# Attention on 64-row halves: another queue for the query blocks, other constants for the side work, other orders of passes and adds

## The chip, the core and the metric

The kernel runs on one core of a Trainium2 chip. A core has TensorE for matrix products (PE in the profile, its weight loads PEld), VectorE (DVE), ScalarE (ACT), GpSimd (POOL) and SyncE (SP), each with an instruction queue of its own that is worked off in order. The metric is the device time of one launch in microseconds (us). The kernel before took 2493.73 us, the median of three runs (2489.62 to 2493.9).

## The reference

Three stages in a row, on u and v of shape 4 x 3072 x 256 and z of shape 4 x 3072 x 64:

```
attn = maximum((1/3072) * z @ z.T, 0) ** 2        # per batch, 3072 x 3072, symmetric
x    = u * (attn @ v)
x    = (h - tanh(h)) @ w_out,  h = x @ w_in       # w_in 256 x 2048
k    = maximum(xk @ w_k, 0) ** 2                  # xk, xr mix x with its row before
out  = sigmoid(xr @ w_r) * (k @ w_v)              # w_k 256 x 1024
```

All weights come as 64-bit floats. Products have single precision: each operand is split into a high part (rounded to TensorE's float format) and a low part (the rest), and every product is three passes, high x high, high x low, low x high.

## The kernel before

The diff touches only the attention stage. It works through 24 tiles t of 512 queries: batch b = t // 6, block g = t % 6. A tile has 12 units p = 0 to 11 (counted through, n = 12 t + p, 288 in all), each for two blocks of 128 keys.

A **fresh** unit computes its scores (`score`, 6 matmuls of 64 rows: two row halves of the array, which run side by side), then `square` on ScalarE (relu, square), a high copy h_A (ScalarE, line 89) and a low part l_A = a - h_A (VectorE, line 92). As the attention matrix is symmetric, a fresh unit whose key block lies beyond the query block is also kept: VectorE transposes it (k, line 660) and SP stores it (at). A **repeated** unit has no scores: `again_load` (line 689, four DMAs on SP) brings a stored block b back, `again_high` (line 700) makes the high part h_t on ScalarE, `produce` the low part l_t on VectorE. Block g has 2 g repeated units; their places stand in a table (`rrfrrrrrfrrr` for g = 5, r repeated, f fresh).

`consume` then adds attn @ v into four accumulators in PSUM: 24 matmuls a unit, two for each (j, c, n), with j one of two key blocks, c one of two column halves, n the pass. The pass n = 1 reads the low part of the unit; passes 0 and 2 its high part. A unit is consumed two units after its scores (LAG = 2, line 56). At the end of a tile the four accumulators have to be emptied before the next tile may write them: `x1_add` (line 1223) copies one half on ScalarE and adds the other on VectorE (both write xs), once for each c; it is handed to `produce` of the next tile's unit p = 1.

The order on every queue is that of the program text, unit by unit: `begin(n)` issues the loads registered for slot n, then scores of unit n, consume of unit n - 2, produce of unit n, the high part of unit n + 1 if it is repeated, and side work. Loads on SP: u of a tile (`u_load`, 8 DMAs, transposing, slot 12 t + 1, or 12 t - 7 where g = 5), the tile's queries q (`ask`, line 148, 8 DMAs of 64 KB each, slot 12 t - 5; only the scores read them), the stored blocks b (five units ahead of their first use), v, z, and the 64-bit weights c.

Side work is spread by a planner, `run_steps` (line 1405), which runs once a unit: in a fresh unit on VectorE between the square and the low part, in a repeated one after the low part. Each task has a first unit, a last unit and steps with costs in us: the conversion of each piece of a 64-bit weight (25 pieces in turn, 4 steps of 1.7, 1.7, 1.2 and 1.5, its load three units before its first unit), transposes of u (1.1), products with u (1.3), splits of v (a ScalarE copy and 1.3) and of z (1.0). A unit has a credit of 2.0, less 1.4 at p = 1 and less 1.0 in a repeated or 1.1 in a kept unit. Steps run while the credit is above zero, and regardless of it when a task has reached its last unit; what is overdrawn is carried on to the next unit.

After the attention, two feed-forward stages run on full 128-row matmuls; GpSimd issues transfers with addition for them.

Of the kernel before, what the change touches and what calls it, by code (L numbers as in the profile page):

```python
# [19 lines left out]
def relu2_attention__tanh_ffn__channel_mix_kernel(  # L20
# [23 lines left out]
    nc = tc.nc  # L44
# [4 lines left out]
    DC = D // P  # L49
    NG = S // TB  # L50
    NT = B * NG
    NP = S // (2 * P)
# [3 lines left out]
    LAG = 2  # L56
# [15 lines left out]
    def p2(name, dt=F32, n=512):  # L72
        return sb.tile([P, n], dt, tag="p2", name=name, bufs=NG + 7)
# [17 lines left out]
    def sub_lo(o, i, hi):  # L91
        nc.vector.tensor_tensor(out=o, in0=i, in1=hi.bitcast(F32), op=ALU.subtract)  # L92
# [55 lines left out]
    def ask(t):  # L148

        b, g = divmod(t, NG)  # L150
        w = asks[t] = [p2(f"q{t}_{l}", F32R) for l in range(2)]
        for l in range(2):
            for d in range(2):
                for h in range(2):
                    nc.sync.dma_start(
                        out=w[l][d * DQ : (d + 1) * DQ, h * 256 : (h + 1) * 256].bitcast(F32),
                        in_=keys[b, g][l][h * DQ : (h + 1) * DQ].bitcast(F32),
                    )
# [475 lines left out]
    def square_split(name, w, sc, high, beside, a, adds):  # L634
        a = a or scratch(f"a_{name}")
        h, l = parts(name)
        square(a, w, sc, adds)
        beside(a)
        high(h, a)
        sub_lo(l, a, h)  # L640
        return h, l
# [3 lines left out]
    for g, order in enumerate(  # L645
        ("ffffffffffff", "ffffrfrfffff", "fffrfrffrffr", "frfrfrfrfrfr", "rrfrfrrfrrfr", "rrfrrrrrfrrr")
    ):
        left = {"r": list(range(2 * g)), "f": list(range(2 * g, NP))}
# [5 lines left out]
    def keep(n, b, g, kp, a):  # L654


        def turn():
            st["t"] = t = p4(f"k{b}_{g}_{kp}", shape=(P, 4, 4, 2, 32))
            for c in range(2):
                nc.vector.transpose(  # L660
                    out=t[:, :, :, c].rearrange("p b a j -> p a b j"),
                    in_=a[:, c].rearrange("p (a b i) -> p a b i", a=4, b=4),
                )

        def store():
            t = st["t"]
            rows = kept[b, g, kp // 2][kp % 2 * P : (kp % 2 + 1) * P, :]
            nc.sync.dma_start(out=rows, in_=t.rearrange("p b a c j -> p (b a c j)"))
            stored.add((b, g, kp))

        st = {}
        if later(n):
            task(n + 3, n + (7 if n < 4 else 9), lambda: [(1.3, turn), (0.0, store)])
        else:
            turn()
            stores[n + 1] = store
# [3 lines left out]
    def wide(n):  # L680
        if n // 2 not in wides:
            wides[n // 2] = sb.tile([P, 2, 2, 512], F32, tag="big", name=f"a_A0_{n}", bufs=12)
        return wides[n // 2][:, n % 2]

    def later(n):

        return 2 <= n < NP
# [128 lines left out]
    def produce(unit, w, adds):  # L816
        kind, t, p = unit
        name = f"{kind}{t}_{p}"
        n = at[unit]
        if n in turned:  # L820
            views, split[unit] = turned.pop(n)
            for hj, lj, xj in views:
                sub_lo(lj, xj, hj)
            for f in adds:
                f()
            return
        b, g = divmod(t, NG)
        kp = pairs[g][p]
        kept_on = (b, g, kp // 2) in kept

        def beside(a):
            run_steps(n)
            if kept_on and not later(n):
                keep(n, b, g, kp, a)

        a = wide(n) if later(n) and kept_on else None
        split[unit] = square_split(
            name, w, scale,
            nc.vector.tensor_copy if not n // NP and n % 2 else copy_hi, beside, a, adds,
        )  # L840
        if kept_on and later(n):
            keep(n, b, g, kp, a)

    def get_acc(kind, t):
        if (kind, t) not in acc:
            acc[kind, t] = [
                ps.tile([P, 512], F32, tag="acc", name=f"acc_{kind}{t}_{c}", bufs=2 * DC)
                for c in range(2 * DC if kind == "A" else DC)
            ]
        return acc[kind, t]  # L850

    def consume(unit):
        for f in pieces_of(unit):
            f()

    def pieces_of(unit):
        kind, t, p = unit
        s = split.pop(unit)
        o = get_acc(kind, t)
        last = NP - 1  # L860
        w = []
        for j in range(2):
            f = 2 * p + j
            kp = pairs[t % NG][p]
            f = kp // 2 * 4 + kp % 2 + 2 * j
            w.append([vs[t // NG, f // 4][:, l, f % 4] for l in range(2)])
        order = [(j, c, n) for j in range(2) for c in range(DC) for n in range(3)]
        if unit == units[0]:
            order = [(j, c, n) for j, n in ((0, 0), (0, 2), (0, 1), (1, 0), (1, 2), (1, 1)) for c in range(DC)]
        elif unit in units[1 : NP - 1]:  # L870
            q = (0, 1, 2) if unit == units[2] else (0, 2, 1)
            order = [(j, c, n) for n in q for j in range(2) for c in range(DC)]
        elif p in (0, last):
            order = [(j, c, n) for c in range(DC) for n in range(3) for j in range(2)]
        whole = at[unit] >= NA - LAG

        def one(j, c, n):

            a, m = PASSES[n]
            for r in (slice(0, P),) if whole else (slice(0, DQ), slice(DQ, P)):  # L880
                nc.tensor.matmul(  # L881
                    o[c if r.start else DC + c],
                    w[j][a][r, c * P : (c + 1) * P],
                    s[m][r, j],
                    start=p == 0 and j == 0 and n == 0,
                    stop=p == last and j == 1 and n == 2
                    or bool(r.start) and at[unit] == NA - LAG - 1 and j == 1 and n == 2,
                )

        return [lambda x=x: one(*x) for x in order]  # L890
# [370 lines left out]
    def load(n, f, *args):  # L1261
        loads.setdefault(max(n, 0), []).append(lambda: f(*args))
# [6 lines left out]
    def task(first, last, steps, *args):  # L1269
        tasks.append([last, first, len(tasks), steps, args])  # L1270
# [3 lines left out]
            load(2 * g - 5, z_load, 0, g)  # L1274
        load(2 * g - 4, v_load, 0, g)
    for t in range(NT):
        n = t * NP + (-7 if t % NG == NG - 1 else 1 if t else 5)
        load(n, u_load, t)
        task(n + 5 if t else NP - 1, t * NP + NP, u_steps, t)
        if t:  # L1280
            load(t * NP - 5, ask, t)
        if t < NT - 1:
            task(t * NP + NP + LAG, t * NP + NP + LAG + 3, x1_steps, t)
    for b in range(1, B):
        prev = (b - 1) * NG * NP
        last = prev + (NG - 1) * NP
        for g in range(NG):
            n = last + LAG + (-18, -6, 3, 6, 9, 11)[g]
            load(n, v_load, b, g)
            task(n + 3, min(n + 12, b * NG * NP + 2 * g + LAG - 2), v_steps, b, g)  # L1290
        for g in range(NG):
            n = prev + 2 * NP + 7 * g
# [6 lines left out]
    order = [(k, g) for g in range(F1 // 512) for k in ("in", "out")]  # L1299
# [4 lines left out]
    for n, x in enumerate(halves):  # L1304
        k = c0 + n * (c1 - c0) // len(halves)
# [13 lines left out]
    for s in range(2):  # L1319
        n = last - 42 + 6 * s  # L1320
# [11 lines left out]
    n = NA + 3 * NHF + 2  # L1332
    load(n, lambda: half_load("ks", *[wd["k", g][:, h] for g in range(2) for h in range(2)]))
    task(n + 1, n + 5, ksum_steps)
    n = NB
# [22 lines left out]
    for i in range(NT // 2):  # L1358
        n = NA + NHF * i
        load(n - 7 if i else n - 18, x_load, i)  # L1360
        task(n - 6 if i else n - 14, n - 1 if i else n - 5, x_steps, i)
    for i in range(NT // 2):
        n = NB + (NK + 1) * i
# [31 lines left out]
    for k in range(8):  # L1395
        t, c, n = NT - 1 - k // 4, k // 2 % 2, NB + (NK + 1) * (k + 1)
# [6 lines left out]
    ready, spare, now = [], [0.0], [0]  # L1403

    def run_steps(n):
        now[0] = n
        for x in [x for x in tasks if x[1] <= n]:
            tasks.remove(x)
            ready.append((x[0], list(x[3](*x[4]))))
        ready.sort(key=lambda x: x[0])  # L1410
        kind = units[min(n, len(units) - 1)][0]
        left = {"A": 2.0, "S": 1.7, "K": 0.0}[kind] + spare[0]
        if kind == "A":
            t, q = divmod(n, NP)
            j = pairs[t % NG][q] // 2 - t % NG
            left -= 1.4 if q == LAG - 1 else 0.0
            left -= 0.3 if later(n) else 1.0 if j < 0 else 1.1 if j > 0 else 0.0
        while ready and (left > 0 or ready[0][0] <= n):
            for x in list(ready):
                if left > 0 or x[0] <= n:  # L1420
                    cost, f = x[1].pop(0)
                    f()
                    left -= cost
                    if not x[1]:
                        ready.remove(x)
        spare[0] = min(left, 0.0) if kind == "A" else max(min(left, 0.0), -0.8)

    with tc.manual_schedule():
        z_load(0, 0)
# [48 lines left out]

        rooms("ps_h")
        q = [f for u in units[NA - LAG : NA] for f in pieces_of(u)]  # L1480
        rest = q[-6:] + [f for cost, f in x1_steps(NT - 1)]
        q = q[:-6]
        for n, (L, i, j) in enumerate(seq):
            begin(slot(n))
            h_unit(n, q)
            q = rest + h_queue(n)
            rest = []
            if L == "K" and j == NK - 1:
# [6 lines left out]
                q = h_piece(n, 0, 0) + q[6:]  # L1495
        n = len(seq) - 1
        c11, c12, c22, c21 = q[:6], q[6:12], q[12:], h_piece(n, 1, 0)
        c21[-1] = with_out(c21[-1], n, 0)
        q = c12[:3] + c22[:3] + c12[3:] + c22[3:] + c11[:3] + c21[:3] + c11[3:] + c21[3:]
# [34 lines left out]
```

## Time and profile before

| | |
|---|---|
| median of 3 runs | 2493.73 us (2489.62 to 2493.9) |
| profiled execution | 2496.21 us, span 2494.3 us, granted clock 0.993 |
| PE, DVE, ACT, POOL busy | 98%, 79%, 76%, 10% of the span |

The profile is of one execution. "Busy" is the union of an engine's instructions; L12 is line 12 of the kernel; out<-in names the tiles written and read; the engine or DMA after "<-" in a wait is what ended it. PEclk is the granted share of TensorE's clock.

### The profile page before, as it was taken

What the parts mean: (1) busy time and instruction counts of PE and PEld (TensorE: products, weight loads), DVE (VectorE), ACT (ScalarE), POOL (GpSimd) and SP (SyncE); (2) the same over time, 40 slices, a digit from 0 to 9 for tenths busy, and PEclk for the clock granted to TensorE, in tenths of its full rate; (3) what the DMA queues carried; (4) which work ended last, traced back from release to release, by engine and by line L of the source; (5) the groups of instructions that cost most, each with busy time, mean ns of one, the idle gap of its engine ahead of it and who ended that gap; (6) DMA issues with size and microseconds to landing.
All of it is one profiled execution on the core that took longest, in us unless ns stands there. A gap on an engine that the chain in (4) does not pass through costs nothing.

```text
span 2494.3 us, 38956 instructions
## 1 busy us (share of the span) xinstructions
PE 2455.3 (98%) x14648; PEld 2026.6 (81%) x14648; DVE 1968.1 (79%) x2746; ACT 1906.8 (76%) x2562; POOL 242.4 (10%) x314
## 2 busy tenths in 40 slices
PE   9999999999989999999999999999999999999998
PEld 7788788778778887888888888888888888888887
DVE  8887888688778877777777777777778778878877
ACT  8765886588568767778777877777777888888886
POOL 0000000000000000022222212221222000000100
PEclk9999999999999999999999999999999999999999
DMA  6888588868877993155665556555667454445733
GB/s 184 245 225 215 185 223 211 215 191 230 206 208 245 258 243 113 39 94 114 144 144 99 112 123 127 109 107 118 127 127 166 138 131 115 114 126 131 160 108 71
DMA packets 447757, 389.39 MB, mean 156 GB/s; under 512 B 261328, under 2 KB 359120, under 8 KB 447568
## 3 DMA queue, kind: packets, MB, share of 16 engines
q1 hardware_dynamic: 395856, 310.67, 44.0%
q0 software_dynamic: 45888, 75.51, 18.9%
q8 instruction: 115, 1.88, 0.3%
q10 hardware_dynamic: 5824, 0.72, 0.2%
q14 instruction: 74, 0.61, 0.1%
HBM read 225.58 MB, written 199.48 MB: 170 GB/s over the span
## 4 chain that ended last, share of the span: by engine, by line
PE 87%; DVE 4%; DMA 3%; ACT 2%; SPq 1%; issue 1%; DVEq 0%; ACTq 0%
PE acc_A L881 23%; PE acc_H L938 21%; PE wa L901 16%; PE we L901 12%; PE acc_K L938 10%; PE w_A L724 3%; DMA b<-at 2%; PE wa_r L901 1%; DVE l_A L92 1%; DVE l_t L92 1%; PE we_q L901 1%; SPq L207 1%; ACT a_A L630 1%; DVE k L660 1%; ACT a_A L627 0%
## 5 line engine op out<-in xcount | busy, mean ns | idle before, releaser
L881 PE MATMUL acc_A<-h_A,v 64*128 64x512 f32 x2688 | 466.6, 390 | 2.4 <-DVE xs L1231 1.4
L881 PE MATMUL acc_A<-h_t,v 64*128 64x512 f32 (+1 forms) x1904 | 352.7, 393 | 16.6 <-ACT xs L1229 8.4
L881 PEld LDWEIGHTS acc_A<-h_A,v 64*128 64x128 f32 x2688 | 312.5, 186 | 54.8 <-DVE xs L1231 4.6
L881 PE MATMUL acc_A<-l_A,v 64*128 64x512 f32 x1344 | 307.1, 392 | 11.2 <-DVE l_A L92 11.1
L881 PEld LDWEIGHTS acc_A<-h_t,v 64*128 64x128 f32 (+1 forms) x1904 | 256.1, 188 | 56.6 <-DVE xs L1231 10.9
L627 ACT ACTIVATE a_A<-w_A 128x1024 f32<-128x1024 f32 (+1 forms) x169 | 171.9, 1017 | 124.6 <-PE w_A L724 123.8
L938 PE MATMUL acc_H<-h_Hy,w_out 128*128 128x512 f32 x768 | 263.9, 389 | 0.0
L881 PE MATMUL acc_A<-l_t,v 64*128 64x512 f32 (+1 forms) x952 | 255.1, 393 | 0.5 <-DVE l_t L92 0.5
L938 PE MATMUL acc_H<-h_Hx,w_out 128*128 128x512 f32 x768 | 252.2, 389 | 0.0
L901 PE MATMUL wa<-xo_T,w_in 128*128 128x512 f32 x864 | 242.8, 389 | 0.4 <-DVE rc L1038 0.4
L92 DVE TENSOR_TENSOR l_A<-a_A,h_A 128x1024 fp32r<-128x1024 f32 (+1 forms) x169 | 201.5, 1192 | 28.6 <-ACT h_A L89 27.9
L89 ACT ACTIVATE h_t<-b 128x512 fp32r<-128x512 f32 x240 | 136.7, 619 | 102.5 <-PE acc_A L881 60.0
L881 PEld LDWEIGHTS acc_A<-l_A,v 64*128 64x128 f32 x1344 | 172.0, 186 | 42.0 <-DVE l_A L92 17.6
L660 DVE STREAM_TRANSPOSE k<-a_A 128x512 f32<-128x512 f32 x240 | 155.6, 688 | 59.2 <-ACT a_A L630 59.0
L1004 DVE TENSOR_TENSOR r<-we,r 128x512 f32<-128x512 f32 x144 | 99.5, 691 | 125.9 <-PE we L901 84.6
L1164 POOL DMA_DIRECT2D mixd<-far x48 | 48.6, 1012 | 1519.3 <-ACT far L1161 1519.3
L1038 DVE TENSOR_TENSOR rc<-we,rc 128x512 f32<-128x512 f32 x144 | 99.3, 689 | 119.1 <-PE we L901 83.3
L901 PEld LDWEIGHTS wa<-xo_T,w_in 128*128 128x128 f32 x864 | 162.0, 188 | 34.8 <-DVE rc L1038 1.3
L630 ACT ACTIVATE a_A<-a_A 128x1024 f32<-128x1024 f32 (+1 forms) x169 | 178.5, 1056 | 5.0
L92 DVE TENSOR_TENSOR l_Hy<-g_H,h_Hy 128x1024 fp32r<-128x1024 f32 x144 | 175.5, 1218 | 7.1 <-ACT h_Hy L89 5.2
L92 DVE TENSOR_TENSOR l_Hx<-g_H,h_Hx 128x1024 fp32r<-128x1024 f32 (+1 forms) x145 | 175.5, 1210 | 3.6 <-ACT h_Hx L89 2.4
L911 ACT ACTIVATE g_H<-rc 128x1024 f32<-128x1024 f32 x96 | 101.8, 1061 | 96.9 <-DVE rc L1038 95.9
(256 smaller groups left out, 5823.7 us busy)
## 6 DMA issues: line engine op xcount, KB each, us to landing
at<-k SPq DMA_DIRECT2D x120, 512.0 KB, 4.5
b<-at SPq DMA_DIRECT2D x240, 256.0 KB, 6.3
timed<-mixd POOLq DMA_DIRECT2D x144, 256.0 KB, 5.4
mixd<-own SPq DMA_DIRECT2D x96, 256.0 KB, 2.0
mx_T<-timed SPq DMA_DIRECT2D x96, 256.0 KB, 4.6
mx_B<-mixd SPq DMA_DIRECT2D x72, 256.0 KB, 4.9
uin<-in_u_dram SPq DMA_DIRECT2D x192, 64.0 KB, 3.2
x1d<-uT SPq DMA_DIRECT2D x24, 512.0 KB, 3.9
```

What stands on the lines that cost most here:

```text
L89: nc.scalar.activation(out=o, in_=i, func=ACTF.Copy)
L92: nc.vector.tensor_tensor(out=o, in0=i, in1=hi.bitcast(F32), op=ALU.subtract)
L627: nc.scalar.activation(out=a, in_=w, func=ACTF.Relu, scale=sc)
L630: nc.scalar.activation(out=a, in_=a, func=ACTF.Square)
L660: nc.vector.transpose(out=t[:, :, :, c].rearrange("p b a j -> p a b j"), in_=a[:, c].rearrange("p (a b i) -> p a b i", a=4, b=4),)
L724: nc.tensor.matmul(o[j], lhsT, asks[t][PASSES[k][1]][r], start=k == 0, stop=k == 2)
L881: nc.tensor.matmul(o[c if r.start else DC + c], w[j][a][r, c * P : (c + 1) * P], s[m][r, j], start=p == 0 and j == 0 and n == 0, stop=p == ...
L901: nc.tensor.matmul(o, w[l], x[m], start=first and k == 0, stop=last and k == 2, skip_group_check=True,)
L911: nc.scalar.activation(out=g, in_=h, func=ACTF.Tanh)
L938: nc.tensor.matmul(o[c], w[a][:, f % 4, c * P : (c + 1) * P], hp[n, half, t][m], start=bool(first and k == 0), stop=bool(last and k == 2),)
L1004: nc.vector.tensor_tensor(out=r1, in0=e, in1=r1, op=ALU.add)
L1038: nc.vector.tensor_tensor(out=rc[:, k], in0=x, in1=rc[:, k], op=ALU.add)
```

## The change

The eight DMAs of `ask` go from SP's queue to GpSimd's. In `produce`, a repeated unit that carries the tile-end adds issues add, low part, add, low part, in place of low part, low part, add, add. In `pieces_of`, units p = 1 to 10 (from tile 1 on) run all high x high products of the unit first, then those with its low part, then those with the low part of v; before, the three passes of one (j, c) followed each other. The load of u for the last block of a batch moves from slot 12 t - 7 to 12 t - 9, and its transpose's first unit with it. In the planner the deduction at p = 1 falls from 1.4 to 1.0, that of a repeated unit from 1.0 to 0.75, and in the attention at most 2.0 of debt is carried on.

```diff
@@ ask @@
-                    nc.sync.dma_start(
+                    nc.gpsimd.dma_start(
                         out=w[l][d * DQ : (d + 1) * DQ, h * 256 : (h + 1) * 256].bitcast(F32),
                         in_=keys[b, g][l][h * DQ : (h + 1) * DQ].bitcast(F32),
                     )
@@ produce @@
             views, split[unit] = turned.pop(n)
-            for hj, lj, xj in views:
+            for k, (hj, lj, xj) in enumerate(views):
+                for f in adds[k : k + 1]:
+                    f()
                 sub_lo(lj, xj, hj)
-            for f in adds:
-                f()
             return
@@ pieces_of @@
-        order = [(j, c, n) for j in range(2) for c in range(DC) for n in range(3)]
+        order = [(j, c, n) for n in range(3) for j in range(2) for c in range(DC)]
@@ loads and tasks @@
-        n = t * NP + (-7 if t % NG == NG - 1 else 1 if t else 5)
+        n = t * NP + (-9 if t % NG == NG - 1 else 1 if t else 5)
         load(n, u_load, t)
         task(n + 5 if t else NP - 1, t * NP + NP, u_steps, t)
@@ run_steps @@
-            left -= 1.4 if q == LAG - 1 else 0.0
-            left -= 0.3 if later(n) else 1.0 if j < 0 else 1.1 if j > 0 else 0.0
+            left -= 1.0 if q == LAG - 1 else 0.0
+            left -= 0.3 if later(n) else 0.75 if j < 0 else 1.1 if j > 0 else 0.0
@@ run_steps, at its end @@
-        spare[0] = min(left, 0.0) if kind == "A" else max(min(left, 0.0), -0.8)
+        spare[0] = max(min(left, 0.0), -2.0) if kind == "A" else max(min(left, 0.0), -0.8)
```

## Rows read from the trace of the kernel before

**Rows 1.** The page: span, and its part 1 (busy us, share, instructions).
```profile
span 2494.3 us, 38956 instructions
...
PE 2455.3 (98%) x14648; PEld 2026.6 (81%) x14648; DVE 1968.1 (79%) x2746; ACT 1906.8 (76%) x2562; POOL 242.4 (10%) x314
```
**Rows 2.** Chain of waits in order of time: start, us, engine, tile, line, instructions.
```profile
54.48 5.44 PE acc_A L881 x48
```
**Rows 3.** Windows: stretch, length, busy us and instructions by engine, clock, DMA share, GB/s.
```profile
10.00:951.00 941.00, 911.02 (x7826) 752.91 (x7826) 770.68 (x1115) 693.15 (x816) 0.00 (x0) 0.98 0.81 220
...
195.00:225.00 30.00, 27.00 (x222) 23.26 (x220) 21.11 (x35) 13.96 (x21) 0.00 (x0) 0.94 1.01 255
435.00:465.00 30.00, 24.40 (x170) 18.13 (x168) 16.48 (x29) 10.28 (x18) 0.00 (x0) 0.83 1.04 247
680.00:710.00 30.00, 22.36 (x174) 17.65 (x172) 17.69 (x29) 12.10 (x20) 0.00 (x0) 0.83 1.02 243
...
93.00:108.00 15.00, 12.93 (x101) 10.32 (x99) 11.91 (x18) 7.89 (x10) 0.00 (x0) 0.89 0.79 187
291.00:306.00 15.00, 12.71 (x98) 10.75 (x97) 12.21 (x18) 9.30 (x12) 0.00 (x0) 0.89 0.31 123
534.00:549.00 15.00, 12.69 (x100) 10.24 (x98) 12.20 (x18) 9.29 (x12) 0.00 (x0) 0.89 0.31 123
...
130.00:140.00 10.00, 8.61 (x75) 6.83 (x73) 7.90 (x11) 5.69 (x8) 0.00 (x0) 1.00 0.72 146
```
**Rows 4.** Waits of PE, 10 to 951 us: releaser, total us, times, longest.
```profile
PE acc_A L881 <- DVE l_A L92: 11.1, 9, 2.3
PE acc_A L881 <- DVE xs L1231: 9.6, 5, 4.5
```
**Rows 5.** Timeline of SP's queue, tiles 10 and 16: start, us to issue all.
```profile
416.36 3.33 SPq L694 DMA_DIRECT2D b<-at  x4
419.73 10.07 SPq L207 DMA_DIRECT2D uin<-in_u_dram  x8
...
430.38 4.95 SPq L155 DMA_DIRECT2D q<-z  x8
435.43 2.04 SPq L694 DMA_DIRECT2D b<-at  x4
...
655.87 0.46 SPq L232 DMA_DIRECT2D c_k<-in_moe_w_k_dram  x1
```
**Rows 6.** Timeline of ACT, tiles 10, 11 and 16; in brackets its idle time.
```profile
427.91 1.15 ACT L89 ACTIVATE h_t<-b 128x512 fp32r<-128x512 f32 x2 [1.19 <-PE acc_A L881]
428.97 1.05 ACT L89 ACTIVATE v<-vr 128x1024 fp32r<-128x1024 f32 x1
...
433.46 1.06 ACT L89 ACTIVATE h_A<-a_A 128x1024 fp32r<-128x1024 f32 x1
...
444.15 2.19 ACT L89 ACTIVATE h_t<-b 128x512 fp32r<-128x512 f32 x4 [8.59 <-DMA b<-at]
...
656.21 1.06 ACT L630 ACTIVATE a_A<-a_A 128x1024 f32<-128x1024 f32 x1
```
**Rows 7.** Timeline of PE: a fresh unit's start in tile 10; tile 16's fifth unit.
```profile
436.33 0.61 PE L881 MATMUL acc_A<-h_A,v 64*128 64x512 f32 x2
...
661.08 0.61 PE L881 MATMUL acc_A<-l_A,v 64*128 64x512 f32 x2
```
**Rows 8.** Timeline of DVE in tile 7: first of seven conversion instructions; l_A.
```profile
290.18 0.42 DVE L267 TENSOR_SCALAR c_in<-cw_in 128x512 int32<-128x512 int32 x1
...
295.44 1.18 DVE L92 TENSOR_TENSOR l_A<-a_A,h_A 128x1024 fp32r<-128x1024 f32 x1
```
**Rows 9.** Line 1164 on POOL: duration in ns, min/median/max; its landing.
```profile
L1164 POOL DMA_DIRECT2D mixd<-far x48: 858/870/2071, 1052.7 to 2306.3; - x48
...
DMA to landing us min/median/max: 3.9/4.2/7.4
```
**Rows 10.** DMA issues: KB each, median us to landing.
```profile
c_k<-in_moe_w_k_dram SPq DMA_DIRECT2D x4, 512.0 KB, 6.7
```

## The prediction

> **What bounds the kernel now.** I read the page's busy shares first: PE is busy 98% of the span, so only time in which PE waits or runs slowly can be won [rows 1]. A busy PE says little of its pace, so next comes the chain of waits, for the pace: 48 matmuls of the weighted sum in 5.44 us, 0.1133 us each when nothing is late [rows 2]. A repeated unit (24 matmuls) thus costs 2.72 us, a fresh one (30) 3.40. Then the windows, because they count matmuls: the length less 0.1133 us per matmul, plus 0.35 for the three that both edges count, is lost time. The attention stretch, 941 us with 7826 matmuls, lost 54.7 us [rows 3]. The diff touches nothing of the later stages, so this is all there is to win.
>
> Where it lies: the three windows around the starts of tiles 5, 11 and 17 (the last query block of a batch) lost 5.2, 11.1 and 10.6, together 26.9 [rows 3]. Three 15 us windows in tiles 2, 7 and 13 lost 3.9, 4.2 and 4.0, together 12.1; the window at tile 3's start 1.85 [rows 3]. The waits name the releasers: xs (the copies and adds that free the accumulators) for the first kind, l_A (the low part of a fresh unit) for the second, 11.1 us in nine waits, the longest 2.3 [rows 4]. Three long ones make about 6.9 of that; the other six add 4.2. In these windows the granted clock is 0.83 to 0.94 where other stretches have 1.00: after each long wait PE runs a while at the lower of its two levels (1.2 GHz), so a wait of 2.3 costs about 4 [rows 3, 4]. The remaining 9.6 us is crumbs, which I leave alone.
>
> The xs waits begin on SP. Ahead of tile 11 the queue issues eight transfers of u (10.07 us), eight of q (4.95) and only then the stored block b (ends 437.47) [rows 5]. ACT, in order, sits 8.59 us on that b before it can reach the xs copies behind it [rows 6]. While the eight q issue, nothing else can be issued, so every load behind them is 5 us late.
>
> **The change part by part.**
>
> *q by GpSimd.* SP loses 4.95 us of issue per tile in front of the b loads [rows 5]. GpSimd, which has no work in the stretch (POOL x0) [rows 3], gets eight DMAs. The trace has no such load there, so I bound it by the DMAs that it issues later: median 0.87, longest 2.07 us, landing 4.2 us after issue [rows 9]. At the median, 8 x 0.87 + 4.2 = 11.2 us, under the shortest five units of notice, 5 x 2.72 = 13.6: cost nothing. At the longest 20.8 us: 7.2 late. I take the median, as most rows lie at it. Nothing else is queued on GpSimd; only the scores of the tile's first fresh unit wait for q.
>
> The row shows VectorE and these DMAs side by side without harm in the later stages [rows 9]. The Trainium skill (SBUF — State Buffer, section "SBUF: two separate sides") speaks against the move: while VectorE runs a copy or cast that takes the port pair that both share, GpSimd can't write its descriptors, and its advice is to issue from SP or ACT; it gives about 3.1 us for a DMA of 0.62 overlapped so. By that figure eight take 24.8 us, an estimate, and q comes some 15 us late; no run here shows it in the attention stretch.
>
> *u two units earlier before tiles 5, 11, 17, 23.* This moves 10 us of SP issue too. Today the order is b (416.36, for the tenth and twelfth unit of tile 10), then u (419.73) [rows 5]. In slot -9 u passes in front of that b: u from 416.36 to 426.4, b to 428.5, and 6.7 us from the last issue to landing, as for the b of 437.47 that ACT got at 444.15 [rows 5, 6]: 435.2. ACT now starts on it at 427.91, so ACT is 7.3 late; a v copy of 1.05 behind it moves to an earlier unit, 6.2 remain; the next fresh unit's high part, done at 434.52, is wanted at 436.33, a lead of 1.8 [rows 6, 7]. New PE wait: 4.4 us. The same order stands at tiles 4 and 16. Bounds: nothing (if SP gets ahead) to 13.2, three times this; I take 7, as at tile 16 it hides behind the wait two paragraphs on. In return b for tile 11 issues by 430.5 and lands at 437.2, while ACT, late itself, asks at about 440: the 8.59 us wait goes. So do those of tiles 5 and 17. Of the 26.9 I keep 1.0 for the accumulators' own hand-over: -25.9, +7.
>
> *Side work spread.* I followed the planner's rule (the list of steps, their costs and due units) through all units, with the old and the new constants. With the old ones it puts three conversion steps (1.7, 1.2, 1.5) due at once into the third unit of tiles 2, 7 and 13; the trace has them in tile 7 from 290.18 on, and l_A of that unit only at 295.44 [rows 8]. The new constants give 120 repeated units 0.25 more and 24 tile ends 0.4 more, some 40 units of cost, and forgive debt beyond 2.0; after tile 0 no unit then gets more than 2.7, and no fresh unit whose block is kept more than 1.7. Total VectorE work is unchanged. The l_A waits go but for 1.5: 16.3 (12.1 + 4.2) less 1.5 is -14.8.
>
> Earlier work needs its data earlier. A conversion's load has three units of notice. At tile 16 the list now puts a z step and the first step of a c conversion into the fifth unit (before: the eleventh). That c load leaves SP at 655.87, behind u, z and b, and lands 6.7 us on (the median for it), at 662.6 [rows 5, 10]. VectorE reaches the step after the square, at 657.3 [rows 6], waits, then needs 1.5 for the step and 1.2 for l_A: 665.3. PE, with high passes first, wants l_A four slots into the unit, at 661.08 [rows 7]. That is 4.2, about 6 with the slow clock behind it. Three more such loads (tiles 5, 11, 17) end on repeated units with more lead; 1 together. Bounds of all these: 0 to 9. I take +7.
>
> *High passes first.* The low part is wanted at the fifth slot of twelve instead of the second, 3 x 0.227 = 0.68 us later; the number of matmuls and weight loads is the same. Taken alone it is worth up to 0.68 in each of nine waits, 5 us; with the bursts gone it only covers what is left, and is in the 1.5 above. The other half of a repeated unit's high part is wanted 0.9 us earlier: nothing while ACT leads by over 1 us.
>
> *Adds interleaved.* In blocks 3 to 5 the first add passes one half-width subtract on VectorE, the second also: each up to 0.7 sooner. That and u's transpose no longer sharing a unit with two steps take most of tile 3's 1.85: -1.4. In the other order a subtract waits behind an add that waits for PE; the unit that needs it starts a whole unit later, so nothing.
>
> **Sum.** 25.9 + 14.8 + 1.4 = 42.1 gone; 7 + 7 = 14 new: 28.1 less. The profiled execution took 2496.21 us (span 2494.3), the median shown is 2493.73; from the median: 2465.
>
> **The rivals.**
> A. The new waits stay away (SP, rid of q, is far enough ahead that u passes without making b late, and c lands in time). For it: the share of the DMA engines is below 1 over the whole stretch, 0.81 [rows 3]. Against: the q of this tile stands behind its u, not ahead of it [rows 5]. 2493.7 - 42 = 2452.
> B. The DMA engines, not SP, set when b lands: their share is 1.01 to 1.04 in the windows of tiles 5, 11, 17 [rows 3]. Then only half of 25.9 comes: 2465 + 13 = 2478. Against: a 5 us hole while q issues.
> C. Bursts move rather than go, since VectorE is 82% busy in the stretch (770.68 of 941) [rows 3]: the 14.8 shrinks to a couple: 2478.
> D, the other side: q late. It decides from 1.18 us per GpSimd DMA, (13.6 - 4.2) / 8. At the longest row, 2.07 us, q is 7.2 late in the 15 tiles whose first unit is fresh: 108 us, 2493.7 + 108 - 28 = 2574; 1.6 us each would still give 51 and end at about 2517. For it: new load on GpSimd beside a busier VectorE. Against: the median 0.87. By the figure that the Trainium skill gives (SBUF — State Buffer, above) it would end past 2574; no row here bears that out.
>
> **How the numbers follow.** Forecast 0.52, A 0.20, B 0.13, C 0.07, D 0.08. About 0.2% (5 us) is what a measurement of this kernel tells from no change. Forecast, A, B and C end below 2489 but for 0.05 in their tails, where more new waits come than I count: faster 0.87, same 0.05, slower 0.08. The range goes from A less some crumbs, 2447, to B with both new terms at their upper bounds, 2485.
>
> **What would show it.** Right: no q on SP and eight DMAs of about 0.9 us per tile on POOL; the windows at tiles 5, 11, 17 near 265 matmuls in 30 us (30 / 0.1133) with clock 1.00; no l_A wait of 2 us in tiles 2, 7, 13; a new ACT wait on b late in tiles 4 and 10, and a VectorE wait on c in tile 16. Wrong: w_A matmuls that wait for q at tile starts (D); xs waits at tile 11 of over 4 us (B); l_A waits elsewhere summing to 10 (C).

## The result, and the profile after

The changed kernel took 2460.89 us (median of 4, 2458.88 to 2462.69) against 2493.26 for the one before on the same chip (median of 4, 2489.62 to 2493.9): ratio 0.9873, 95% interval 0.9856 to 0.989, 32.4 us less. The forecast was 28 less. The profiled executions stand at 2496.21 before and 2462.35 after, 33.9 less, and it is these two that the rows compare.

First the page's span and its part 1, then the windows (columns as in [rows 3]), which answer to [rows 1] and [rows 3]:

```profile
span 2460.6 us, 39117 instructions
PE 2440.0 (99%) x14648; PEld 2037.7 (83%) x14648; DVE 1966.2 (80%) x2746; ACT 1908.6 (78%) x2562; POOL 338.1 (14%) x498
```
```profile
10.00:920.00 910.00, 898.70 (x7851) 765.48 (x7852) 770.55 (x1117) 697.40 (x820) 94.34 (x184) 0.99 0.83 228
...
190.00:220.00 30.00, 30.00 (x268) 24.77 (x266) 26.30 (x42) 18.75 (x27) 7.71 (x16) 1.00 1.10 280
415.00:445.00 30.00, 26.49 (x214) 21.26 (x212) 20.82 (x33) 17.21 (x25) 5.54 (x11) 0.98 1.10 273
660.00:690.00 30.00, 29.82 (x261) 24.34 (x259) 22.67 (x37) 18.95 (x28) 6.14 (x13) 1.00 1.07 277
628.00:658.00 30.00, 24.31 (x196) 20.27 (x194) 19.41 (x32) 14.34 (x19) 5.72 (x12) 0.89 0.94 226
...
93.00:108.00 15.00, 15.00 (x135) 14.20 (x133) 14.86 (x23) 11.69 (x14) 0.00 (x0) 1.00 0.76 226
290.00:305.00 15.00, 15.00 (x136) 12.40 (x134) 12.87 (x17) 12.34 (x13) 0.00 (x0) 1.00 0.59 187
528.00:543.00 15.00, 15.00 (x136) 13.26 (x134) 13.99 (x21) 13.84 (x14) 0.00 (x0) 1.00 0.94 270
...
126.00:136.00 10.00, 10.00 (x91) 10.00 (x89) 9.12 (x15) 7.26 (x10) 0.00 (x0) 1.00 0.93 195
```

Read as before, the attention stretch lost 910 - 7851 x 0.1133 + 0.35 = 20.8 us, where it had lost 54.7 [rows 3]: 33.8 less, the whole gain. The windows around the starts of tiles 5, 11 and 17 (second to fourth line) lost 0, 6.1 and 0.8 where they had lost 5.2, 11.1 and 10.6; the three in tiles 2, 7 and 13 and the one at tile 3's start lost nothing. Most of what is left lies in two places: 6.1 in the window of tile 11, and 30 - 196 x 0.1133 + 0.35 = 8.1 in a new one, 628 to 658, in tile 16, where the kernel before lost nothing. There the granted clock is 0.89; around the long waits before it was 0.83 to 0.94 [rows 3].

The waits of PE in this stretch (as in [rows 4]), the waits of VectorE on transfers, and four rows of VectorE's timeline name them:

```profile
PE acc_A L881 <- DVE l_A L92: 7.0, 4, 5.7
PE acc_A L881 <- DVE l_t L92: 2.4, 1, 2.4
PE acc_A L881 <- DVE xs L1231: 1.7, 4, 0.7
```
```profile
DVE cw_out L253 <- DMA c_out<-in_moe_w_out_dram: 10.2, 3, 5.8
DVE cw_k L253 <- DMA c_k<-in_moe_w_k_dram: 9.0, 2, 7.6
DVE zt L127 <- DMA zin<-in_z_dram: 2.4, 2, 2.0
```
```profile
403.93 0.43 DVE L253 TENSOR_SCALAR cw_out<-c_out 128x512 int32<-128x512 int32 x1 [2.81 <-DMA c_out<-in_moe_w_out_dram]
...
440.73 0.43 DVE L253 TENSOR_SCALAR cw_out<-c_out 128x512 int32<-128x512 int32 x1 [5.81 <-DMA c_out<-in_moe_w_out_dram]
...
637.74 0.43 DVE L253 TENSOR_SCALAR cw_k<-c_k 128x512 int32<-128x512 int32 x1 [7.63 <-DMA c_k<-in_moe_w_k_dram]
639.15 1.22 DVE L92 TENSOR_TENSOR l_A<-a_A,h_A 128x1024 fp32r<-128x1024 f32 x1
```

[Rows 4] show half of the waits on xs in the kernel before, those for VectorE (9.6); the copies on ScalarE held PE as well:

```profile
PE acc_A L881 <- ACT xs L1229: 8.4, 3, 4.0
```

Together the waits on xs fell from 18.0 to 1.7. In their place stand VectorE's waits on c: the conversion step now comes before the data. In tile 16 the low part l_A of that unit stands right behind the step, and PE waits 5.7 us for it. The one wait on l_t, 2.4 us, is tile 11's.

SP's queue and ScalarE in tile 10 (columns as in [rows 5] and [rows 6]):

```profile
397.57 10.05 SPq L207 DMA_DIRECT2D uin<-in_u_dram  x8
407.73 3.92 SPq L694 DMA_DIRECT2D b<-at  x8
...
413.07 3.89 SPq L108 DMA_DIRECT2D zin<-in_z_dram  x4
...
429.72 0.40 SPq L238 DMA_DIRECT2D c_out<-in_moe_w_out_dram  x1
...
629.15 0.45 SPq L232 DMA_DIRECT2D c_k<-in_moe_w_k_dram  x1
```
```profile
415.54 1.15 ACT L89 ACTIVATE h_t<-b 128x512 fp32r<-128x512 f32 x2 [6.99 <-DMA b<-at]
418.73 1.06 ACT L89 ACTIVATE h_A<-a_A 128x1024 fp32r<-128x1024 f32 x1
...
419.70 2.17 ACT L89 ACTIVATE h_t<-b 128x512 fp32r<-128x512 f32 x4
```

No q stands between u and b any more, and u passes in front of b, as the edit says. ScalarE's 8.59 us wait ahead of tile 11 [rows 6] is gone (the h_t at 419.70 starts without one), and a new one of 6.99 stands in tile 10, on the b that u passed.

### The profile page after: what moved, and what is told of

It reads as the page before. It is cut to its first block, busy times and chain, and to the rows that moved or that the text cites. A ratio compares the mean times of both kernels' runs of the same rounds, so it can differ in the third digit from the quotient of the medians.

```text
span 2460.6 us, 39117 instructions
## 1 busy us (share of the span) xinstructions
PE 2440.0 (99%) x14648; PEld 2037.7 (83%) x14648; DVE 1966.2 (80%) x2746; ACT 1908.6 (78%) x2562; POOL 338.1 (14%) x498
## 4 chain that ended last, share of the span: by engine, by line
PE 93%; DMA 2%; DVE 2%; ACT 1%; SPq 1%; issue 0%; POOL 0%; DVEq 0%; POOLq 0%
PE acc_A L881 27%; PE acc_H L938 21%; PE wa L901 16%; PE we L901 12%; PE acc_K L938 10%; PE w_A L724 4%; PE wa_r L901 1%; PE we_q L901 1%; DMA c_out<-in_moe_w_out_dram 1%; DMA vr<-in_v_dram 0%; DMA b<-at 0%; SPq L207 0%; ACT a_A L630 0%; ACT a_A L627 0%; DMA c_k<-in_moe_w_k_dram 0%
## 5 line engine op out<-in xcount | busy, mean ns | idle before, releaser
L881 PE MATMUL acc_A<-h_A,v 64*128 64x512 f32 x2688 | 392.7, 387 | 1.1 <-DVE h_A L776 0.7
L881 PEld LDWEIGHTS acc_A<-h_A,v 64*128 64x128 f32 x2688 | 284.7, 184 | 46.9 <-DVE h_A L776 1.1
L881 PE MATMUL acc_A<-h_t,v 64*128 64x512 f32 (+1 forms) x1904 | 281.1, 388 | 1.7 <-DVE xs L1231 1.7
L881 PEld LDWEIGHTS acc_A<-h_t,v 64*128 64x128 f32 (+1 forms) x1904 | 205.6, 185 | 34.1 <-DVE xs L1231 3.3
L881 PE MATMUL acc_A<-l_A,v 64*128 64x512 f32 x1344 | 202.1, 389 | 7.0 <-DVE l_A L92 7.0
L155 POOL DMA_DIRECT2D q<-z x184 | 95.0, 525 | 669.9 <-PE w_A L724 333.5
L89 ACT ACTIVATE h_A<-a_A 128x1024 fp32r<-128x1024 f32 x161 | 170.7, 1060 | 4.2
L938 PEld LDWEIGHTS acc_H<-h_Hy,w_out 128*128 128x128 f32 x768 | 144.2, 188 | 30.1 <-ACT h_Hy L89 0.2
```

The costliest lines, as they stand in the source:

```text
L89: nc.scalar.activation(out=o, in_=i, func=ACTF.Copy)
L881: nc.tensor.matmul(o[c if r.start else DC + c], w[j][a][r, c * P : (c + 1) * P], s[m][r, j], start=p == 0 and j == 0 and n == 0, stop=p == ...
L938: nc.tensor.matmul(o[c], w[a][:, f % 4, c * P : (c + 1) * P], hp[n, half, t][m], start=bool(first and k == 0), stop=bool(last and k == 2),)
```

## Experiments

Each edit is to the kernel before (the first three) or to the changed one. All compute the whole result.

**The three parts alone.** First the queue of q, nothing else.

```diff
@@ ask, in the kernel before @@
-                    nc.sync.dma_start(
+                    nc.gpsimd.dma_start(
```


> The kernel before, with q's eight DMAs on GpSimd as the only edit. Theory (q's 4.95 us of issue on SP made b late): the ACT wait on b ahead of tile 11 falls from 8.59 to 2 to 4 us, the windows of tiles 5, 11 and 17 lose 5 to 9 us together in place of 26.9, about 2474 us in all (-19). Rival 1 (u's earlier load did it): less than 4 us are won, 2489 or more. Rival 2 (the DMA engines set when b lands): b lands as late as before, 2490 or more.

Measured: 2477.34 us against 2491.82, ratio 0.9932 (0.992 to 0.9944): 14.5 less, nearer to the theory than to either rival, but short of it. The three windows lose 13.9, where 5 to 9 were expected. The trace says which tile is missing:

```profile
430.00:460.00 30.00, 25.34 (x178) 19.15 (x176) 17.18 (x29) 11.44 (x19) 2.14 (x4) 0.83 1.05 248
```
```profile
432.88 2.19 ACT L89 ACTIVATE h_t<-b 128x512 fp32r<-128x512 f32 x4 [4.57 <-DMA b<-at]
```
```profile
438.01 0.45 DVE L127 STREAM_TRANSPOSE zt<-zin 128x256 f32<-128x256 f32 x1 [8.14 <-DMA zin<-in_z_dram]
```

With q off SP the wait on b ahead of tile 11 is 4.57 instead of 8.59, and at tile 5 the window of 190 to 220 is full (x268). At tile 17 the window of 670 to 700 has 235 matmuls, a loss of 3.7. But tile 11 still loses 10.2 (the first line): u is in its old slot, in front of tile 11's z, and VectorE waits 8.14 us for z. The queue edit frees tile 5 and most of 17, and hardly helps tile 11.

Then the planner's three constants alone.

```diff
@@ run_steps, in the kernel before @@
-            left -= 1.4 if q == LAG - 1 else 0.0
-            left -= 0.3 if later(n) else 1.0 if j < 0 else 1.1 if j > 0 else 0.0
+            left -= 1.0 if q == LAG - 1 else 0.0
+            left -= 0.3 if later(n) else 0.75 if j < 0 else 1.1 if j > 0 else 0.0
...
-        spare[0] = min(left, 0.0) if kind == "A" else max(min(left, 0.0), -0.8)
+        spare[0] = max(min(left, 0.0), -2.0) if kind == "A" else max(min(left, 0.0), -0.8)
```


> The kernel before, with the three planner constants as the only edit. Theory (forced bursts made l_A late): the waits on l_A in tiles 2, 7 and 13 go, worth 12 to 15 us; the early first step of a c conversion brings waits on c at tiles 16 and 11 of some 4 to 8 us; in all -5 to -10, about 2486 us. Rival (the pass order removed the l_A waits): within 2 us of before, 2491 to 2495, apart from the waits on c.

Measured: 2487.55 us, ratio 0.9977 (0.9968 to 0.9985): 4.3 less, just under the low end of what was expected. Its waits:

```profile
PE acc_A L881 <- DVE l_A L92: 13.0, 8, 6.5
```
```profile
DVE cw_k L253 <- DMA c_k<-in_moe_w_k_dram: 9.7, 2, 7.3
```

The bursts go (the window of tile 2 has 129 matmuls, from 101 [rows 3]), and the waits on c come with this edit alone: PE's wait on l_A grows from 11.1 [rows 4] to 13.0, half of it one wait of 6.5. So the late c belongs to the planner, with or without q and u moved. (This profile is of the fastest of eleven executions, 2482.39 us.) The planner alone also clears the start of tile 3, which had lost 1.85 [rows 3]. The window around it has 133 matmuls in 15 us, a loss of 0.3:

```profile
121.00:136.00 15.00, 14.97 (x133) 12.04 (x131) 13.02 (x20) 10.60 (x13) 0.00 (x0) 1.00 0.98 245
```

And the order of the passes alone.

```diff
@@ pieces_of, in the kernel before @@
-        order = [(j, c, n) for j in range(2) for c in range(DC) for n in range(3)]
+        order = [(j, c, n) for n in range(3) for j in range(2) for c in range(DC)]
```


> The kernel before, with the pass order as the only edit. Theory: each of the nine l_A waits shrinks by at most 0.68 us, so 5 us, up to 8 with the slow clock behind them; 2485 to 2489 us, and waits of 1.6 us stay in tiles 2, 7 and 13. Rival (the pass order removes the l_A waits): -14 or more, 2479 or less.

Measured: 2485.72 us, ratio 0.9972 (0.9962 to 0.9982): 6.1 less, as expected. PE's waits on l_A go from 11.1 us in nine, the longest 2.3 [rows 4], to 5.1 in five, about the 0.68 that the low part gains in each of nine. They do not vanish:

```profile
PE acc_A L881 <- DVE l_A L92: 5.1, 5, 1.3
```

**Parts taken back.** u at its old slot, all else changed:

```diff
@@ loads and tasks, in the changed kernel @@
-        n = t * NP + (-9 if t % NG == NG - 1 else 1 if t else 5)
+        n = t * NP + (-7 if t % NG == NG - 1 else 1 if t else 5)
```


> The changed kernel, with u of the last block loaded in slot 12 t - 7 again. Theory (u two units earlier passes in front of b and beside c, and is a cost): the ACT wait of 6.99 us on b in tile 10 falls below 2 us, c of tile 16 lands about 2 us sooner, tile 11 starts no later; 2 to 6 us faster than the changed kernel, about 2457. Rival (the earlier u is part of what freed b of tiles 5, 11 and 17): 5 to 12 us slower, 2466 or more.

Measured: 2464.15 us, ratio 0.9886 (0.9873 to 0.9899); the changed kernel stood at 0.9873 and 0.9864 on two chips. It was expected to be faster, and it was not: the theory that u's move costs more than it gives fell. It is some 3 us slower, short of the rival's 5. The wait on b in tile 10 shrank from 6.99 to 2.82 (below 2 was expected), but z, now behind u, came late to tiles 5 and 11:

```profile
198.54 0.45 DVE L127 STREAM_TRANSPOSE zt<-zin 128x256 f32<-128x256 f32 x1 [4.70 <-DMA zin<-in_z_dram]
...
429.80 0.45 DVE L127 STREAM_TRANSPOSE zt<-zin 128x256 f32<-128x256 f32 x1 [4.61 <-DMA zin<-in_z_dram]
```

What u passes in slot -9 is b, which had slack; what it passes in slot -7 is z, which had none. The price shows at tile 5: 222 matmuls in the window of 190 to 220, a loss of 5.2 where the changed kernel loses none. Tile 11 loses 4.6 (227 in 418 to 448), no more than the 6.1 of the changed kernel. With the queue edit alone tile 5 was free with u in the same old slot, so the late z there comes with the other edits; which of them is not isolated. The wait on c_k in tile 16 stayed (6.90), so u's place is not its cause.

The order of the passes as before:

```diff
@@ pieces_of, in the changed kernel @@
-        order = [(j, c, n) for n in range(3) for j in range(2) for c in range(DC)]
+        order = [(j, c, n) for j in range(2) for c in range(DC) for n in range(3)]
```


> The changed kernel with the pass order of before. Theory (with the bursts gone the pass order only covers what is left): 1 to 4 us slower than the changed kernel, 2462 to 2465, as the low part is wanted 0.68 us sooner in a few late units. Rival (the pass order is what removed the l_A waits): 10 us slower or more, 2471.

Measured: 2465.22 us, ratio 0.9884 (0.9867 to 0.99); the changed kernel, run again on the same chip beside it, was 3.8 faster (below). The intervals overlap; the direction and the size are those expected. PE's waits on l_A are 9.0 us, from 7.0:

```profile
PE acc_A L881 <- DVE l_A L92: 9.0, 6, 5.5
```

The added ones are short: 0.6 and 0.7 more in tile 10, and 0.4 each in tiles 7 and 13, where the changed kernel has none.

q back on SP, all else changed:

```diff
@@ ask, in the changed kernel @@
-                    nc.gpsimd.dma_start(
+                    nc.sync.dma_start(
```


> The changed kernel with q's eight DMAs on SP again. Theory (q on SP is what makes b and z late at tiles 5, 11, 17): 12 to 20 us slower than the changed kernel, about 2475 to 2480, with xs waits at these starts. Rival (with the other edits in place the queue hardly matters): within 5 us, 2461 to 2466.

Measured: 2471.15 us, ratio 0.9909 (0.9893 to 0.9926): some 10 us of the gain are gone, less than expected. The profiled execution, the fastest of the four, shows 5 of them. The windows of tiles 5, 11 and 17 have 223, 231 and 261 matmuls in 30 us, losses of 5.1, 4.2 and 0.8: tile 5 is late again, tiles 11 and 17 are no later than in the changed kernel. A further 3.6 lies in tile 4 (148 matmuls in 180 to 200 us), where l_A stands behind a late c_out and PE waits 3.2 us; it is one of these three:

```profile
PE acc_A L881 <- DVE l_A L92: 9.5, 3, 5.6
```

The longest, 5.6, is the wait for c_k in tile 16. PE stands there shortly before tile 17 starts, and that may be what gives the loads of tile 17 their time; the last experiment below has q on SP without that wait, and tile 17 is late again.

The tile-end adds as before:

```diff
@@ produce, in the changed kernel @@
-            for k, (hj, lj, xj) in enumerate(views):
-                for f in adds[k : k + 1]:
-                    f()
+            for hj, lj, xj in views:
                 sub_lo(lj, xj, hj)
+            for f in adds:
+                f()
```


> The changed kernel with the tile-end adds behind both low parts again. Theory (each first add passes 0.65 us of subtracts in twelve tiles, of which few are late): 0 to 2 us slower than the changed kernel, 2461 to 2463. Rival (the adds alone made tile 3's start late and others with it): 3 us slower or more.

Measured: 2463.23 us, ratio 0.9875 (0.986 to 0.989), not told apart from the changed kernel. Whether the order of the adds is worth anything stays open; by the medians it is some 2 us. At tile 3's start, which the forecast gave to the adds, 132 matmuls stand in 121 to 136 us: a loss of 0.4, not the 1.85 of the kernel before.

**The changed kernel again**, on the chip of the next two experiments and of the order of the passes above (no edit):

> The changed kernel once more, as the measure for the other three on this chip: 0.987 of before, about 2461 us. The same waits as in its first profile: 8 us in the fifth unit of tile 16 and 4 us in tile 11, both behind a c load, if they are the schedule's own; rival (chance of one execution): at other places.

Measured: 2461.43 us, ratio 0.9864 (0.9849 to 0.9879). PE's waits are those of the first profile, so they are the schedule's own: 5.1 us for l_A in tile 16 and 2.1 for l_t in tile 11.

```profile
PE acc_A L881 <- DVE l_A L92: 6.5, 2, 5.1
PE acc_A L881 <- DVE l_t L92: 2.1, 1, 2.1
```

**Loads sooner.** The c loads three units earlier:

```diff
@@ loads and tasks, in the changed kernel @@
-        load(k - 3, c_load, *x)
+        load(k - 6, c_load, *x)
```


> The changed kernel, with each 64-bit weight piece loaded six units ahead of its first step in place of three. Theory (the planner's earlier first step waits for its load): the 8 us at tile 16 and the 4 us at tile 11 go, 9 to 12 us less than the changed kernel, about 2450. Rival (the DMA engines are full there, a transfer that comes sooner only delays a b): at most 3 us less, and waits on b in tiles 11 and 16 instead.

Measured: 2453.46 us, ratio 0.9834 (0.982 to 0.9849), 8.0 below the changed kernel on the same chip; expected were 9 to 12. The windows of tile 16 (628 to 658) and tile 11 (415 to 445) go from 196 and 214 matmuls to 247 and 267: both places of loss were the c loads. But the window of tile 5, which was full, now loses 6.0 (x215), and VectorE waits for z:

```profile
190.00:220.00 30.00, 26.36 (x215) 22.86 (x213) 25.24 (x41) 16.75 (x25) 4.32 (x9) 0.94 1.09 274
```
```profile
DVE zt L127 <- DMA zin<-in_z_dram: 5.2, 3, 2.5
```

The rival is right in part: ScalarE's waits on b rise from 21.7 to 27.9 us, one of 5.2 just ahead of tile 5. z was moved too, from three units of notice to six:

```diff
@@ loads and tasks, on top of the c edit @@
-            load(n - 3, z_load, b, g)
+            load(n - 6, z_load, b, g)
```


> As the kernel with c loaded sooner, and z too, six units ahead of its steps in place of three. Theory (z too is waited for, at the starts of tiles 5 and 11): another 1 to 3 us less, about 2448, and no wait on z of over 2 us on VectorE in tiles 4 and 10. Rival (full DMA engines): no less than with c alone, or more, 2450 to 2455.

Measured: 2445.96 us, ratio 0.9806 (0.9791 to 0.982): another 7.5, more than expected, and the fastest of all versions. Tile 5 is full again (x269), which is where most of the 7.5 lies. The attention stretch and PE's waits in it:

```profile
10.00:905.00 895.00, 894.05 (x7856) 773.13 (x7857) 772.07 (x1120) 698.00 (x822) 94.69 (x184) 1.00 0.85 231
```
```profile
PE acc_A L881 <- DVE xs L1231: 0.6, 2, 0.4
PE acc_A L881 <- DVE l_A L92: 0.3, 1, 0.3
```

It loses 895 - 7856 x 0.1133 + 0.35 = 5.3 us in all: PE is the bound of the whole stretch now, and no wait is worth more than 0.4 us.

With the loads sooner, is the rest of the change still needed? u back, and q back on SP, each on top of it (the edits as above):

> The kernel with c and z loaded sooner, with u of the last block in slot 12 t - 7 again. Theory (u's earlier slot helped by letting z, behind it on SP, land before VectorE wants it): now that z comes sooner anyway, within 2 us of the kernel with c and z sooner, 2444 to 2448. Rival (u's earlier slot frees b or u itself): 3 us slower or more, 2449.

Measured: 2451.63 us, ratio 0.9825 (0.9811 to 0.984). Expected was no difference beyond 2; the medians differ by 5.7 (on two chips, on which the kernel before stands within 0.2 us), and the intervals just overlap. The profiled executions differ by 3.2 us, and the trace shows where: at tiles 5, 11 and 17, with 168, 294 and 256 matmuls in 220 to 240, 425 to 460 and 670 to 700 us, against 180, 312 and 268 with u in its new slot. VectorE waits for no z in either, and ScalarE's waits on b are 34.0 us against 29.4. So u's place seems not to be indifferent even with z in time, as the rival has it: some 3 us by the profiles and 5.7 by the medians. With intervals that overlap the size stays open.

> The kernel with c and z loaded sooner, with q on SP again. Theory (SP's issue time in front of b): 5 to 12 us slower than with q on GpSimd, 2451 to 2458, with waits of ACT on b ahead of tiles 5, 11 and 17. Rival (what q delayed on SP was mostly z and c): within 3 us, 2446 to 2449.

Measured: 2464.57 us, ratio 0.9878 (0.9863 to 0.9893): 18.6 of the gain gone, more than expected. ScalarE's waits on b, with q on GpSimd and with q on SP, and what PE then waits for:

```profile
ACT h_t L89 <- DMA b<-at: 29.4, 13, 4.0
```
```profile
ACT h_t L89 <- DMA b<-at: 44.5, 13, 6.4
```
```profile
PE acc_A L881 <- ACT xs L1229: 7.6, 4, 2.6
```

PE waits for xs at the starts of tiles 5, 11 and 17 (2.0, 2.6 and 2.4 us on ScalarE's half), as expected, and their windows lose 4.9, 6.0 and 4.6. With c and z late, q on SP had cost tiles 11 and 17 nothing (above). The queue edit is worth 14.5 alone, 10 beside the other parts, 18.6 when the other loads come in time. One at a time the three parts give 14.5 + 4.3 + 6.1 = 25 of the 32 that they give together with u's move and the adds.

## Why the prediction came out right

The total was right (2465 forecast, 2461 measured), and the two largest terms with it. Part of that is luck: the two new waits were forecast at 7 each and came to 1.1 and 13.4, which is nearly the same sum, and two gains came by another edit than the one named.

*Tile starts, -25.9.* The three windows lost 26.9 and now lose 0 + 6.1 + 0.8; of the 6.1, about 4 belongs to tile 11's wait on c (the window of 428 to 446 us, x111, lost 5.8, with 1.8 of it at the tile's start by the gaps between PE's units). That leaves 2.9 of hand-over: -24.0. That q in front of the loads is the reason is shown both ways for tile 5: the queue edit alone frees it, q back on SP makes it late. For tiles 11 and 17 it is shown where c and z come in time: q on SP then costs them 6.0 and 4.6. That u's move is needed as well was in the forecast, but for the wrong load: the text looks at b alone, and the queue edit alone (8.14 us on z) and u put back (4.70 and 4.61 on z) show that z, which the prediction does not name in this step, is what u must pass. With z in time u's place still tells on b, as the experiment with c, z and u shows (waits of 34.0 us against 29.4).

*New wait on b, +7: over-sized.* ScalarE's wait has the forecast size (7.3 forecast, 6.99 measured), but PE's does not: forecast 4.4 in tile 10, while the window of 413 to 428 us, behind that wait, holds 126 matmuls in 15 us and lost 15 - 126 x 0.1133 + 0.35 = 1.1. h_A is done at 418.73 + 1.06 = 419.79 and PE reads it from 419.85 on: it arrived just as it was wanted.

```profile
419.85 1.19 PE L881 MATMUL acc_A<-h_A,v 64*128 64x512 f32 x8
```

The step that failed is the way from b to h_A, in both its ends. First, b was forecast 1.1 us before PE wants h_A (435.2 and 436.33) and came 4.3 before (415.54 and 419.85): SP was further ahead, u leaving it 22.3 us before that read and not 20.0. The wait of 6.99 is as long as forecast only because ScalarE was free sooner too. Second, ScalarE needs 4.25 us from b to the end of h_A, not the 5.6 that the forecast kept (427.91 to 434.52, less the v copy). In the kernel before, 1.29 of that was a wait for PE's scores, which is slack and no work:

```profile
431.31 1.03 ACT L627 ACTIVATE a_A<-w_A 128x1024 f32<-128x1024 f32 x1 [1.29 <-PE w_A L724]
```

*Bursts, -14.8: right.* The three windows lost 12.1 and are full. The planner alone and the passes alone both shrink them, by different means: the planner takes the burst away, the passes hide 0.68 of each wait. With the bursts gone the passes were forecast to be worth little of their own; taken back they cost 3.8 by the medians and 2.0 in the profiles, in the short waits named above. The 4.2 of short waits in this term stood in tiles 8, 12, 18, 19 and 23. In 15 us windows these places lost 6.7 (1.7, 1.1, 1.0, 1.1 and 1.9), and the changed kernel loses nothing there. The planner alone clears the first four (136, 136, 134 and 136 matmuls in 15 us), the queue edit alone the one in tile 23 (136).

*New waits on c, +7: under-sized.* Tile 16 lost 8.1, not 6, and tile 11 about 4, not a share of 1. A third place was not forecast: in tile 10 VectorE waits 2.81 us for c_out at 403.93, has no gap from there to the unit's l_A, and PE waits 0.94 for that; the window of 398 to 413 (x124) lost 1.3. That is 13.4 in all. The step that failed is the landing: the median of 6.7 [rows 10] was taken for loads that go out beside u and z. Here c_k, issued at 629.15, let VectorE start at 637.74, 8.6 us later; c_out, issued at 429.72, at 440.73, 11.0 later (its median is 5.4). That these loads are the cause is shown: asked for three units sooner, tiles 10 and 11 lose nothing to them, tile 16 loses 2.4, and 8 us of the total come back although tile 5 loses 6.0.

*Adds, -1.4.* Tile 3's start lost 1.85 and lost nothing after, but not by the adds: the planner alone leaves 0.3 of it, and with the adds put back 0.4 stands there. The prediction gave this gain to the wrong edit.

*The sum.* By these windows 24.0 + 12.1 + 1.85 + 6.7 = 44.7 are gone, where 42.1 were forecast, and 1.1 + 13.4 = 14.5 are new, where 14 were. That is 30.1 of the 33.8; the other 3.7 come from the crumbs that the forecast left alone (9.6 in all) and are not placed. The range's upper end, B with both new terms at their bounds of 13.2 and 9, adds up to 2487 and not to 2485; nothing hangs on it.

*The rivals.* A (no new waits) is half true: b late costs 1.1, c does cost. B (the DMA engines hold b back) does not hold: tiles 5 and 17 start freely at a DMA share of 1.10 and 1.07, higher than the 1.01 and 1.02 at which they stood before [rows 3]. C (bursts move) does not: waits on l_A are 7.0, of which 5.7 and 0.9 are c loads. D (q late) does not: its DMAs on GpSimd are all short, and no matmul that reads q waits for them (PE's waits above name no q). Line 155 on POOL:

```profile
L155 POOL DMA_DIRECT2D q<-z x184: 518/518/692, 9.3 to 773.8; - x184
...
PE w_A L724: 333.5, 18
...
DMA to landing us min/median/max: 1.8/5.8/7.9
```

The longest, 0.692 us, is under the 1.18 from which D decides, and the second line says that GpSimd waits for PE to free q's buffers: it runs ahead. It stays short although VectorE is busy 770.55 of 910 us.

VectorE does hold these DMAs up, by very little. Five of the 184 took over 0.6 us. One is the first of the launch. In each of the other four VectorE began an instruction of a weight conversion, a TENSOR_SCALAR of 0.42 or 0.43 us, 0.12 to 0.16 us after the DMA did, and the DMA ended 0.11 us after that instruction:

```profile
773.09 0.68 POOL L155 DMA_DIRECT2D q<-z  x1
```
```profile
773.24 0.42 DVE L253 TENSOR_SCALAR cw_v<-c_v 128x512 int32<-128x512 int32 x1
```

Where VectorE ran only transposes and tensor-tensor instructions, or nothing, no DMA but the launch's first took over 0.541 us. The Trainium skill (SBUF — State Buffer, section "SBUF: two separate sides") holds that VectorE, in a two-port mode, locks GpSimd out of the port pair that both share, so that GpSimd cannot write its descriptors until that instruction ends. The trace agrees with such a lock for these instructions; which mode they run in it does not show. The price that the prediction took from the page, 3.1 us a DMA, does not occur: the instruction that holds the DMA up lasts 0.42 us, and the delay is 0.17 us at most (0.691 for 0.518).

## What to carry over

Time that a queue spends on issuing is a cost to every load behind it: read the queue's own timeline and ask which loads must not be passed, all of them and not just the one whose wait the profile names (here b was named and z was next). Side work that is spread more evenly comes earlier, so its loads must go out earlier in the same edit; six units of notice instead of three for c and z turned 2461 into 2446 us. Judge the landing of such a load by the rows in the busiest stretch, not by the median. And check a forecast term by term, each against the run that isolates it: here the total was right while two of its terms were far off in opposite directions.

## What the runs showed of the hardware

The 64 KB load of q holds SP 0.594 us (median; 1.971 at most), and GpSimd 0.518 (0.692 at most); from issue to landing it takes 2.4 us from SP and 5.8 from GpSimd (medians). With the queue as the only edit the landing from GpSimd is 5.5. The queue that is free of other loads is thus the one on which a transfer takes longer, and it pays all the same, since nothing waits for q. Line 155 on SP, in the kernel before:

```profile
L155 SPq DMA_DIRECT2D q<-z x184: 461/594/1971, 21.2 to 910.6; - x184
...
DMA to landing us min/median/max: 1.9/2.4/9.2
```

When a TENSOR_SCALAR of 0.42 us on VectorE begins 0.12 to 0.16 us after a DMA on GpSimd, that DMA lasts until 0.11 us after the TENSOR_SCALAR's end; this happens four times in the changed kernel (0.656 to 0.691 us in place of 0.518).
